# Converting float64 weights with the integer addition and the last subtraction on VectorE instead of GpSimd

## The chip, the cores and the metric

The kernel runs on one core of a Trainium2 chip. The metric is the device time of one execution in microseconds (us); less is better. Engines are named as in the profile: PE is TensorE (matrix products; PEld is its weight load), DVE is VectorE, ACT is ScalarE, POOL is GpSimd, SP is SyncE, which issues all DMAs of this kernel.

## The reference

A two-step attention over packed keys, and then a feed-forward network with a leaky activation, all in float32:

```python
def sm_attn(qq, kk, vv):
    s = scale * np.matmul(qq, kk.transpose(0, 1, 3, 2))
    s = s - np.max(s, axis=-1, keepdims=True)
    a = np.exp(s)
    a = a / (np.sum(a, axis=-1, keepdims=True) + 1e-09)
    return np.matmul(a, vv)
p_packed = sm_attn(p, k, v)            # p: 32 packed queries a head
out = sm_attn(q, p_packed, p_packed)   # back to 576 tokens
...
h = x @ w_in                           # x: out as 4608 tokens x 512
g = np.maximum(h, 0.0) + alpha * np.minimum(h, 0.0)
return (g @ w_out).astype(np.float32)
```

There are 8 batches of 8 heads, 576 tokens, head size 64; the model width is 512, the inner width (`d_ff`) 2048. `w_in` (512 x 2048) and `w_out` (2048 x 512) come as float64 numbers, and the kernel turns them into float32 ones itself.

## The kernel before

Tokens lie on the free axis throughout. `x w_in` is taken as the softmax matrix times `p' w_in`, so that the first product contracts 256 rows. Products are float32 ones made of float32r parts: each operand is split exactly into `hi + lo`, where `hi` is a rounding copy on ACT and `lo` the difference.

**Conversion.** `convert` takes one tile of 128 x 512 float64 numbers from its DMA (`raw`, tile `wraw`) to the pair `hi`, `lo`. There are 32 such units: 16 of `w_in` (made in `packed_w`, result tile `w`, which also goes back to DRAM as `w_split` for later batches) and 16 of `w_out` (made in `load_w_out`, result tile `wo`, which stays). A unit's steps: ACT takes the absolute value of the upper words (L117, `mag`) and scales the lower words to integers (L118, in place in `wraw`); DVE clamps the upper words (L119), moves exponent and fraction to float32's places (L122), and puts the sign on (L128, new tile `full`); POOL adds the lower word as an integer to the bits (L132); ACT makes `hi` (L135); the subtraction that gives `lo` (L137) goes to POOL and to DVE in turn. Raw tiles lie in places of `w_out` that are filled last; four of them rotate. `mag` shares three buffers with the tile `xh`, and `full` three with the tile `xl`, both of `split_x` in the attention.

**Stages.** The first batch's attention comes first, alone. Then the steps of the generators in `plan` are woven into the loop over tiles of the FFN: `first` makes a tile of 128 inner columns by 288 tokens, `second` multiplies it into the four output accumulators two tiles later. In the first batch (32 tiles: both halves over each quarter of `d_ff`) the conversions `w0` and `wo` are woven in, one step of each every two tiles, and DVE makes the activation: `neg` (L490) and `g` (L494) from PSUM. ACT copies `gh` (L505), and `gl` (L507) is the difference, on POOL in the first 48 tiles and on DVE later. Of the attention's other work, POOL has the difference in `split_x` (`xl`, L176), that of v (`vs`, L278), the subtraction of the maximum (L374), the scaling (L381) and `a_l` (L395). Each `g` of the first batch is one instruction of line 494, 32 in all, so their times mark how far the first batch is.

**Order.** The code's order is only a wish: the program is built with a scheduler that reorders the instructions of each engine by its own estimate of times, and then each engine runs its list in order. SP has a list too, so a DMA whose tile is not free holds up those behind it.

Of the kernel before, what the change touches and what calls it, by code (L numbers as in the profile page):

```python
# [8 lines left out]
F32 = mybir.dt.float32  # L9
U32 = mybir.dt.uint32  # L10
U64 = mybir.dt.uint64
F32R = mybir.dt.float32r
AF = mybir.ActivationFunctionType
ALU = mybir.AluOpType
AX = mybir.AxisListType


# Upper words of the float64 numbers 2^-127 and (just under) 2^128, read as float32 numbers.
F64_BOTTOM = float.fromhex("0x1p-15")
F64_TOP = float.fromhex("0x1.dffffep+16")  # L20


def fv(ap):
    """The float32 view of a float32r tile, for reads by the elementwise engines."""
    return ap.bitcast(F32)


# [1 line left out]
def pack_attention_ffn_kernel(  # L29
# [8 lines left out]
    alpha: bass.AP,  # L38
    outT: bass.AP,
):  # L40
    """x = softmax(q p'^T) p' with p' = softmax(p k^T) v, then prelu(x w_in) w_out.

    x w_in is taken as A (p' w_in), A being the softmax over the packed keys, so that
    the first product of the FFN contracts heads * n_pack = 256 rows and not 512.
    Products are float32 ones: each operand is split exactly into two float32r parts
    of 12 significant bits, hi + lo. The small products take all four part products,
    stacked so that they are two passes, the large ones hi*hi + lo*hi + hi*lo.
    Tokens lie on the free axis throughout; the output leaves transposed.
    """
    nc = tc.nc  # L50

    B, NP, P, S = qT.shape
# [13 lines left out]
    xin = ctx.enter_context(tc.tile_pool(name="xin", bufs=3))  # L66
# [3 lines left out]
    at = ctx.enter_context(tc.tile_pool(name="at", bufs=3))  # L70
# [4 lines left out]
    op = ctx.enter_context(tc.tile_pool(name="op", bufs=2))  # L75
# [4 lines left out]

    w_split = dram.tile([NJ, NP, P, 2, 512], F32, name="w_split")

    # ---- constants
    ident = const.tile([P, P], F32, name="ident")
    make_identity(nc, ident)
    ii = const.tile([P, 64], F32, name="ii")
# [6 lines left out]
    pt = const.tile([P, NP, 2, 2, 64], F32R, name="pt")  # L93
# [4 lines left out]
        nc.gpsimd.memset(t, 0.0)  # L98
    wo_t = {}

    turn = [0]
    XF = 1

    def convert(src, raw, place):
        """hi + lo = the float32 nearest to the float64 numbers whose bits are src.

        The upper word carries sign, exponent and 20 bits of the fraction: moved to
        float32's places it is the number cut to 20 bits; 2^exponent times the lower
        word is the rest. The upper word is clamped first to float32's exponents, the
        lowest of which with no fraction stands for zero; sign and top exponent bit do  # L110
        not change by that.
        """
        nc.sync.dma_start(out=raw, in_=src)
        u = raw.bitcast(U32).rearrange("p (f t) -> p f t", t=2)
        up = raw.bitcast(F32).rearrange("p (f t) -> p f t", t=2)[:, :, 1]
        mag = xin.tile([P, 512], F32, name="mag", tag="xh")
        nc.scalar.activation(out=mag, in_=up, func=AF.Abs)  # L117
        nc.scalar.activation(out=u[:, :, 0], in_=u[:, :, 0], func=AF.Copy, scale=2.0**-29)  # L118
        nc.vector.tensor_scalar(  # L119
            out=mag, in0=mag, scalar1=F64_BOTTOM, scalar2=F64_TOP, op0=ALU.max, op1=ALU.min  # L120
        )
        nc.vector.tensor_scalar(  # L122
            out=mag.bitcast(U32), in0=mag.bitcast(U32), scalar1=3, scalar2=0x3FFFFFF8,
            op0=ALU.logical_shift_left, op1=ALU.bitwise_and,
        )
        full = xin.tile([P, 512], F32, name="full", tag="xl")
        bits = full.bitcast(U32)
        nc.vector.scalar_tensor_tensor(  # L128
            out=bits, in0=u[:, :, 1], scalar=0xC0000000, in1=mag.bitcast(U32),
            op0=ALU.bitwise_and, op1=ALU.bitwise_or,  # L130
        )
        nc.gpsimd.tensor_tensor(out=bits, in0=bits, in1=u[:, :, 0], op=ALU.add)  # L132
        hi, lo = place()
        turn[0] += 1
        nc.scalar.copy(out=hi, in_=full)  # L135
        eng = nc.gpsimd if turn[0] % 2 else nc.vector
        eng.tensor_tensor(out=lo, in0=full, in1=fv(hi), op=ALU.subtract)  # L137

    def new_raw(f=0):
        """Room for float64 numbers, in those places of w_out that are filled last."""  # L140
        if f in left:
            left.remove(f)
            n = f
        elif f == NF - 1:
            n = f
        else:
            n = left.pop(0)
            left.append(n)
        return const.tile([P, 512], U64, name=f"wraw{n}", tag=f"wo{n}")
# [9 lines left out]
        raw = new_raw(f)  # L159
        convert(w_out[f * P : (f + 1) * P, :], raw, place)  # L160

    # ---- attention
    def load_x(src, b, pr):
        if b == 0 and (src is kT or pr == NP - 1):
            n = pr if src is kT else 2 * NP
# [24 lines left out]
        return raw  # L190

    def scores(b, pr, st, x, dst, exact):
        """dst[64 rows of this pair] = both heads' scores, keys or tokens on the free axis."""
        ro = (pr % 2) * 64
        for hf in range(2):
            sl = slice(hf * HS, hf * HS + HS)
            if exact:
                if b == 0:
                    tag = f"acc{(2 * pr + hf) % 4}"
                    ps = ps_a.tile([P, 512], F32, name=tag, tag=tag)  # L200
                else:
                    ps = ps_m.tile([P, 512], F32, name="ps_m", tag="m")
                nc.tensor.matmul(ps[:64, :HS], st[:, pr], x[:, sl], start=True, stop=True)
                if hf or b > 0:
                    nc.scalar.copy(out=dst[ro : ro + 64, sl], in_=ps[0:64, :HS])
                else:
                    nc.vector.tensor_copy(out=dst[ro : ro + 64, sl], in_=ps[0:64, :HS])
                continue
            ps = ps_m.tile([P, 512], F32, name="ps_m", tag="m")
            nc.tensor.matmul(ps[:, :HS], st[:, pr], x[0][:, sl], start=True, stop=False)  # L210
            nc.tensor.matmul(ps[:, :HS], st[:, pr], x[1][:, sl], start=False, stop=True)
            lo = sm.tile([64, HS], F32, name="lo", tag="lo", bufs=2)
            nc.scalar.copy(out=lo, in_=ps[64:128, :HS])
            nc.vector.tensor_tensor(
                out=dst[ro : ro + 64, sl], in0=ps[0:64, :HS], in1=lo, op=ALU.add
            )
# [4 lines left out]
        result[b] = (a_h, a_l)  # L221

    def attention(b, tp, exact=False):
        """Steps of two head pairs of a batch; leaves p' in `pt` and the softmax over it in `at`.

        exact takes float32 products as the tensor engine has them: more passes, but no
        splits, for the first batch, before which the tensor engine has nothing to do.
        """
        ptb, slots = (pt0, (0, 1)) if b == 0 else (pt, (b % 2, b % 2))
        pr0, pr1 = prs = (2 * tp, 2 * tp + 1)  # L230
        ts = slice(2 * tp, 2 * tp + 2)
# [1 line left out]
        split = (lambda x: x) if exact else split_x  # L233
# [6 lines left out]
        if tp == 0:  # L240
            for r in range(2):
# [3 lines left out]
                else:  # L245
                    nc.scalar.copy(out=s1[rs, :, 0, cs], in_=praw[rs])
                    nc.vector.tensor_tensor(
                        out=s1[rs, :, 1, cs], in0=praw[rs], in1=fv(s1[rs, :, 0, cs]),
                        op=ALU.subtract,
# [33 lines left out]
        vraw.append(load_v(b, pr1))  # L283
        vs = split_v(0)
        yield
        # rows: keys; columns: pair, (hi, lo), head and packed key
        if exact:
            aT = vin.tile([P, KT, 2, 1, 64], F32, name="aT", tag=("aT", "vs")[tp], bufs=1)
        else:
# [1 line left out]
        for t0 in range(0, KT, 3):  # L291
# [3 lines left out]
            for i in range(n):  # L295
                t = min((t0 + i) * P, S - P)
                nc.tensor.transpose(
                    out=ps[:, i * P : i * P + P], in_=s_t[:, t : t + P], identity=ident
# [3 lines left out]
            if not exact:  # L302
                nc.vector.tensor_tensor(
                    out=aT[:, ks, :, 1, :], in0=psq, in1=fv(aT[:, ks, :, 0, :]), op=ALU.subtract
# [39 lines left out]
        for r in range(2):  # L344
# [3 lines left out]
            else:  # L348
                nc.scalar.copy(out=p2[rs, ts, 0, cs], in_=ppv[rs, :, cs])
                nc.vector.tensor_tensor(  # L350
                    out=p2[rs, ts, 1, cs], in0=ppv[rs, :, cs], in1=fv(p2[rs, ts, 0, cs]),
                    op=ALU.subtract,
                )
        if exact:
            for pr in prs:
                hi, lo = (ptb[:, pr, part, slots[pr % 2], :] for part in range(2))
# [16 lines left out]
        eng = nc.vector if b < 0 else nc.gpsimd  # L373
# [21 lines left out]
        nc.gpsimd.tensor_tensor(out=a_l[:, tp, :], in0=s2, in1=fv(a_h[:, tp, :]), op=ALU.subtract)  # L395
        yield

    # ---- p' w_in for batches of a group, 512 columns of d_ff at a time
    def packed_w(bs, units, fresh=False):
        def get(j, pr):  # L400
            if fresh:
# [48 lines left out]
                ws.append(get(*units[n + LA]))  # L450
            yield

    # ---- FFN of half a batch, one tile of d_ff at a time
    def split_pw(k, h):
        """hi and lo of 256 columns of p' w_in"""
        src = pw[k // 2, h // 2][:, :, (h % 2) * 256 : (h % 2) * 256 + 256]
        th = pwj.tile([P, 2, 256], F32R, name="pwh", tag="pwh")
        tl = pwj.tile([P, 2, 256], F32R, name="pwl", tag="pwl")
        nc.vector.tensor_copy(out=th, in_=src)  # L459
        eng = nc.gpsimd if k < 4 else nc.vector  # L460
        eng.tensor_tensor(out=tl, in0=src, in1=fv(th), op=ALU.subtract)  # L461
        pj[k, h] = (th, tl)
# [117 lines left out]
    for ch in PRO:  # L580
        next(wo if ch == "o" else w0)

    # Work for the gaps: (tile of d_ff from whose loop on it goes, steps, tiles a step)
    A1 = (-1, 6, 19)
    A2 = (17, 20, 30, 34, 40)
    AG = (-8, -5, 12, 15, 30)
# [8 lines left out]
        plan += [(T + AG[n], attention(2 * g + n // 2, n % 2), 1) for n in range(4)]  # L595
        plan += [(T + AG[4], packed_w([2 * g, 2 * g + 1], units(*range(NJ))), 1)]

    # The first batch takes both halves over each quarter of d_ff, whose weights are just then
    # being converted; the others one half after the other over all of it.
    order = [(h, 4 * j + f) for j in range(NJ) for h in range(2) for f in range(4)]  # L600
    order += [(k, f) for k in range(2, 2 * B) for f in range(NF)]
    AHEAD = 2
# [45 lines left out]
```

## Time and profile before

| | before |
|---|---|
| runs, median (lowest to highest) | 849.3 us (848.91 to 850.4) |
| profiled execution, first to last instruction | 849.7 us |
| busy: PE, PEld | 785.0 us (92%), 731.3 us (86%) |
| busy: DVE, ACT, POOL | 661.7 us (78%), 544.3 us (64%), 323.3 us (38%) |
| POOL, additions of the lower word (L132) | 32, 44.2 us |
| POOL, last subtractions into `w` (L137) | 12, 17.8 us |
| moved by DMA | 97.98 MB, mean 115 GB/s |

The profiled execution is one run; its time is its span of 849.7 us, with nothing listed around it, 0.4 us over the median of the three runs. In the rows, "busy" of an engine is the time in which one of its instructions runs, whether that instruction works or stands still; a row of a group gives busy us, mean ns of one, and the idle time ahead with what ended it. A row of the timeline gives the start, the duration and the idle time ahead of it.

### The profile page before, as it was taken

The page shows a single profiled execution, that of the slowest core. Times are in us where ns is not written, and L with a number is a line of the kernel's source. Part 1 is how long each engine was busy: PE and PEld are TensorE (multiplying, and loading weights), DVE is VectorE, ACT ScalarE, POOL GpSimd, SP SyncE. Part 2 cuts the span into 40 slices and gives each one's busy share as a digit, 9 for nine tenths or more (in the row PEclk, how much of TensorE's full clock was granted, in tenths as well). Part 3 has the DMA queues.
Part 4 walks back from the last instruction along what each step waited for, and adds up shares of the span by engine and source line. Part 5 has one row for each costly group of instructions (what it writes and reads, how often), then busy time and mean ns, then how long its engine had stood idle before and what let it go on. Part 6 is the DMA issues. An engine that isn't in the chain of part 4 may idle for free.

```text
span 849.7 us, 15212 instructions
## 1 busy us (share of the span) xinstructions
PE 785.0 (92%) x5384; PEld 731.3 (86%) x5384; DVE 661.7 (78%) x1239; ACT 544.3 (64%) x1333; POOL 323.3 (38%) x299
## 2 busy tenths in 40 slices
PE   5558799998999999999999999998899999999997
PEld 3336668787789999999999999997899999999997
DVE  4999999865788867889989857889889746666663
ACT  5657656547776797666666787656666784545453
POOL 2577768766996621325334402245132100000000
PEclk9869999999999999999999999999999999999999
DMA  8765656445632474222122473221100640000000
GB/s 297 257 225 193 229 188 217 156 145 189 214 109 87 140 244 126 62 57 62 50 59 84 149 234 104 67 70 43 43 15 30 196 154 1 30 1 29 1 30 28
DMA packets 55387, 97.98 MB, mean 115 GB/s; under 512 B 5136, under 2 KB 32784, under 8 KB 55312
## 3 DMA queue, kind: packets, MB, share of 16 engines
q1 hardware_dynamic: 55312, 97.02, 35.6%
q8 instruction: 42, 0.69, 0.3%
q14 instruction: 33, 0.27, 0.1%
HBM read 79.18 MB, written 17.83 MB: 114 GB/s over the span
## 4 chain that ended last, share of the span: by engine, by line
PE 62%; DVE 14%; ACT 5%; issue 3%; DMA 2%; POOL 1%; SPq 0%; DVEq 0%; ACTq 0%; POOLq 0%
PE acc L521 12%; PE acc L519 12%; PE acc L520 12%; PE ps_h L483 6%; PE ps_h L484 5%; PE ps_h L485 5%; DVE g L500 2%; DVE gl L507 2%; DVE pwl L461 2%; DMA outT<-ot 2%; PE ps_m L438 1%; PE ps_m L319 1%; PE ps_m L439 1%; PE ps_m L440 1%; PE ps_m L210 1%
## 5 line engine op out<-in xcount | busy, mean ns | idle before, releaser
L519 PE MATMUL acc<-gh,wo 128*128 128x288 f32 x1024 | 300.5, 302 | 6.3 <-ACT gh L505 2.9
L520 PE MATMUL acc<-gh,wo 128*128 128x288 f32 x1024 | 296.8, 296 | 0.0
L521 PE MATMUL acc<-gl,wo 128*128 128x288 f32 x1024 | 265.3, 298 | 3.7 <-DVE gl L507 2.9
L519 PEld LDWEIGHTS acc<-gh,wo 128*128 128x128 f32 x1024 | 193.4, 189 | 12.9 <-ACT gh L505 3.9
L505 ACT CAST gh<-g 128x288 fp32r<-128x288 f32 x256 | 110.3, 433 | 145.6 <-DVE g L500 105.8
L520 PEld LDWEIGHTS acc<-gh,wo 128*128 128x128 f32 x1024 | 193.5, 189 | 2.2
L521 PEld LDWEIGHTS acc<-gl,wo 128*128 128x128 f32 x1024 | 180.0, 188 | 9.9 <-DVE gl L507 5.0
L507 DVE TENSOR_TENSOR gl<-g,gh 128x288 fp32r<-128x288 f32 x208 | 124.7, 602 | 59.7 <-ACT gh L505 56.5
L500 DVE SCALAR_TENSOR_TENSOR g<-neg,nal,g 128x288 f32<-128x288 f32 x224 | 130.7, 586 | 39.5 <-ACT g L499 38.3
L483 PE MATMUL ps_h<-a_h,pwh 128*128 128x288 f32 x448 | 132.6, 296 | 0.5 <-DVE pwh L459 0.4
L484 PE MATMUL ps_h<-a_l,pwh 128*128 128x288 f32 x448 | 132.0, 295 | 0.0
L485 PE MATMUL ps_h<-a_h,pwl 128*128 128x288 f32 x448 | 131.4, 295 | 0.0
L176 POOL TENSOR_TENSOR xl<-xraw,xh 128x576 fp32r<-128x576 f32 x48 | 72.7, 1514 | 148.5 <-ACT xh L175 144.1
L498 ACT ACTIVATE neg<-ps_h 128x288 f32<-128x288 f32 x224 | 92.2, 412 | 50.4 <-PE ps_h L485 46.6
L499 ACT ACTIVATE g<-ps_h 128x288 f32<-128x288 f32 x224 | 91.0, 408 | 15.0 <-DVE gl L507 13.5
L483 PEld LDWEIGHTS ps_h<-a_h,pwh 128*128 128x128 f32 x448 | 84.2, 188 | 2.0 <-DVE pwh L459 0.7
L484 PEld LDWEIGHTS ps_h<-a_l,pwh 128*128 128x128 f32 x448 | 84.1, 188 | 0.3
L485 PEld LDWEIGHTS ps_h<-a_h,pwl 128*128 128x128 f32 x448 | 83.9, 188 | 0.4
L461 DVE TENSOR_TENSOR pwl<-pw,pwh 128x512 fp32r<-128x512 f32 x96 | 76.1, 793 | 5.7 <-DVE pwh L459 0.5
L459 DVE CAST pwh<-pw 128x512 fp32r<-128x512 f32 x112 | 61.2, 550 | 12.1 <-PE ps_h L484 10.1
L446 ACT COPY pw<-ps_m 64x512 f32<-64x512 f32 x112 | 65.1, 581 | 6.4 <-PE ps_m L440 5.0
L132 POOL TENSOR_TENSOR full<-full,wraw 128x512 uint32<-128x512 uint32 x32 | 44.2, 1382 | 41.2 <-ACT mag L117 14.0
(118 smaller groups left out, 1211.8 us busy)
## 6 DMA issues: line engine op xcount, KB each, us to landing
w<-w_split SPq DMA_DIRECT2D x64, 512.0 KB, 4.1
xraw<-in_kT SPq DMA_DIRECT2D x32, 288.0 KB, 2.9
xraw<-in_qT SPq DMA_DIRECT2D x32, 288.0 KB, 2.9
outT<-ot SPq DMA_DIRECT2D x64, 144.0 KB, 1.8
vraw<-in_v SPq DMA_DIRECT2D x32, 256.0 KB, 2.9
wraw<-in_w_out SPq DMA_DIRECT2D x16, 512.0 KB, 3.7
wraw<-in_w_in SPq DMA_DIRECT2D x16, 512.0 KB, 4.2
w_split<-w SPq DMA_DIRECT2D x16, 512.0 KB, 3.3
```

The source lines that it names most:

```text
L461: eng.tensor_tensor(out=tl, in0=src, in1=fv(th), op=ALU.subtract)
L483: nc.tensor.matmul(ps[:, :HS], th[:, i, fs], a_h[:, i, tok], start=hi, stop=False)
L484: nc.tensor.matmul(ps[:, :HS], th[:, i, fs], a_l[:, i, tok], start=False, stop=False)
L485: nc.tensor.matmul(ps[:, :HS], tl[:, i, fs], a_h[:, i, tok], start=False, stop=lo)
L498: nc.scalar.activation(out=neg, in_=ps[:, :HS], func=AF.Relu, scale=-1.0)
L499: nc.scalar.activation(out=g, in_=ps[:, :HS], func=AF.Relu)
L500: nc.vector.scalar_tensor_tensor(out=g, in0=neg, scalar=nal[:, f : f + 1], in1=g, op0=ALU.mult, op1=ALU.add)
L505: nc.scalar.copy(out=gh, in_=g)
L507: eng.tensor_tensor(out=gl, in0=g, in1=fv(gh), op=ALU.subtract)
L519: nc.tensor.matmul(acc[o][:, :HS], wo_t[f][:, 0, os_], gh, start=begin, stop=False)
L520: nc.tensor.matmul(acc[o][:, :HS], wo_t[f][:, 1, os_], gh, start=False, stop=False)
L521: nc.tensor.matmul(acc[o][:, :HS], wo_t[f][:, 0, os_], gl, start=False, stop=end)
```

## The change

The integer addition moves from POOL to DVE, and all 32 last subtractions are DVE's (16 were). The lower word goes to a tile of its own, `low`, in the buffers that `full` had, instead of being scaled in place; `full` is gone, and `mag` is worked on in place from the absolute value to the last subtraction. The core of the diff (docstrings and comments, which it also takes out, left out here; lines further down move up by three: L490, L494 and L507 are L487, L491 and L504 afterwards):

```diff
-    turn = [0]
...
         mag = xin.tile([P, 512], F32, name="mag", tag="xh")
+        bits = mag.bitcast(U32)
         nc.scalar.activation(out=mag, in_=up, func=AF.Abs)
-        nc.scalar.activation(out=u[:, :, 0], in_=u[:, :, 0], func=AF.Copy, scale=2.0**-29)
+        low = xin.tile([P, 512], U32, name="low", tag="xl")
+        nc.scalar.activation(out=low, in_=u[:, :, 0], func=AF.Copy, scale=2.0**-29)
...
-            out=mag.bitcast(U32), in0=mag.bitcast(U32), scalar1=3, scalar2=0x3FFFFFF8,
+            out=bits, in0=bits, scalar1=3, scalar2=0x3FFFFFF8,
             op0=ALU.logical_shift_left, op1=ALU.bitwise_and,
         )
-        full = xin.tile([P, 512], F32, name="full", tag="xl")
-        bits = full.bitcast(U32)
         nc.vector.scalar_tensor_tensor(
-            out=bits, in0=u[:, :, 1], scalar=0xC0000000, in1=mag.bitcast(U32),
+            out=bits, in0=u[:, :, 1], scalar=0xC0000000, in1=bits,
             op0=ALU.bitwise_and, op1=ALU.bitwise_or,
         )
-        nc.gpsimd.tensor_tensor(out=bits, in0=bits, in1=u[:, :, 0], op=ALU.add)
+        nc.vector.tensor_tensor(out=bits, in0=bits, in1=low, op=ALU.add)
         hi, lo = place()
-        turn[0] += 1
-        nc.scalar.copy(out=hi, in_=full)
-        eng = nc.gpsimd if turn[0] % 2 else nc.vector
-        eng.tensor_tensor(out=lo, in0=full, in1=fv(hi), op=ALU.subtract)
+        nc.scalar.copy(out=hi, in_=mag)
+        nc.vector.tensor_tensor(out=lo, in0=mag, in1=fv(hi), op=ALU.subtract)
```

The scheduler lays the lists anew. In the rows that follow, a number behind `wraw` or `wo` tells one unit's tile from another's. POOL's list from the last copy of the constants on, its first rows before:

```order
L88 COPY ii<-ident 64x64
L132 TENSOR_TENSOR full<-full,wraw_320 128x512
L132 TENSOR_TENSOR full<-full,wraw_333 128x512
L137 TENSOR_TENSOR wo_330<-full,wo_330 128x512
L132 TENSOR_TENSOR full<-full,wraw_347 128x512
L132 TENSOR_TENSOR full<-full,wraw_366 128x512
L137 TENSOR_TENSOR w<-full,w 128x512
L374 TENSOR_TENSOR t_273<-t_273,m_275 128x576
L132 TENSOR_TENSOR full<-full,wraw_380 128x512
L137 TENSOR_TENSOR wo_390<-full,wo_390 128x512
```

and after, down to the first `gl`:

```order
L88 COPY ii<-ident 64x64
L371 TENSOR_TENSOR t_273<-t_273,m_275 128x576
L371 TENSOR_TENSOR t_308<-t_308,m_310 128x576
L378 TENSOR_TENSOR t_273<-t_273,z_288 128x576
L378 TENSOR_TENSOR t_308<-t_308,z_314 128x576
L504 TENSOR_TENSOR gl<-g,gh 128x288 x9
```

Eleven additions and five subtractions stand ahead of the first `gl` before; after, four steps of the attention alone do, and nine of the `gl` follow each other.

DVE's list up to the first `g`, before:

```order
L119 TENSOR_SCALAR mag<-mag 128x512
L122 TENSOR_SCALAR mag<-mag 128x512
L386 STREAM_TRANSPOSE a_f<-t_308 128x576
L137 TENSOR_TENSOR w<-full,w 128x512
L128 SCALAR_TENSOR_TENSOR full<-wraw_460,mag 128x512
L119 TENSOR_SCALAR mag<-mag 128x512
L122 TENSOR_SCALAR mag<-mag 128x512
L490 TENSOR_SCALAR neg<-ps_h,al 128x288
L128 SCALAR_TENSOR_TENSOR full<-wraw_478,mag 128x512
L494 SCALAR_TENSOR_TENSOR g<-ps_h,neg 128x288
```

and after, where `ISA` is the addition of line 131, listed as 1024 elements a partition (the 512 words as halves), and L120, L123, L127 and L134 are the former L119, L122, L128 and L137:

```order
L134 TENSOR_TENSOR w<-mag,w 128x512
L127 SCALAR_TENSOR_TENSOR mag<-wraw_447,mag 128x512
L134 TENSOR_TENSOR w<-mag,w 128x512
L131 ISA mag<-mag,low 128x1024
L120 TENSOR_SCALAR mag<-mag 128x512
L487 TENSOR_SCALAR neg<-ps_h,al 128x288
L120 TENSOR_SCALAR mag<-mag 128x512
L123 TENSOR_SCALAR mag<-mag 128x512
L487 TENSOR_SCALAR neg<-ps_h,al 128x288
L134 TENSOR_TENSOR wo_457<-mag,wo_457 128x512
L491 SCALAR_TENSOR_TENSOR g<-ps_h,neg 128x288
```

Before, eleven units have their sign (L128) ahead of the first `g`; after, nine have, and nine additions and nine subtractions stand there with them, where four subtractions did.

DVE's list up to the 13th `g`, before:

```order
L137 TENSOR_TENSOR wo_881<-full,wo_881 128x512
L128 SCALAR_TENSOR_TENSOR full<-wraw_976,mag 128x512
L490 TENSOR_SCALAR neg<-ps_h,al 128x288
L119 TENSOR_SCALAR mag<-mag 128x512
L494 SCALAR_TENSOR_TENSOR g<-ps_h,neg 128x288
L122 TENSOR_SCALAR mag<-mag 128x512
L128 SCALAR_TENSOR_TENSOR full<-wraw_1060,mag 128x512
L490 TENSOR_SCALAR neg<-ps_h,al 128x288
L119 TENSOR_SCALAR mag<-mag 128x512
L494 SCALAR_TENSOR_TENSOR g<-ps_h,neg 128x288
```

and after:

```order
L127 SCALAR_TENSOR_TENSOR mag<-wraw_839,mag 128x512
L123 TENSOR_SCALAR mag<-mag 128x512
L120 TENSOR_SCALAR mag<-mag 128x512
L131 ISA mag<-mag,low 128x1024
L127 SCALAR_TENSOR_TENSOR mag<-wraw_871,mag 128x512
L123 TENSOR_SCALAR mag<-mag 128x512
L487 TENSOR_SCALAR neg<-ps_h,al 128x288
L131 ISA mag<-mag,low 128x1024
L134 TENSOR_TENSOR w<-mag,w 128x512
L127 SCALAR_TENSOR_TENSOR mag<-wraw_944,mag 128x512
L491 SCALAR_TENSOR_TENSOR g<-ps_h,neg 128x288
```

Ahead of the 13th `g` there stood 24 of L119, 23 each of L122 and L128 and 10 of L137; now there stand 21, 21 and 21 of these, 20 additions and 19 subtractions. Ahead of the 32nd, all 32 units are through DVE's steps on either side. Shortly behind the 32nd, from DVE's row 280 of before (329 of after) on, the two lists agree; so do those of PE, ACT and SP from places near it.

## The prediction

> **What bounds the kernel now.** First the page's slices, which show the change's stage, then busy times by stretch, then what PE waits for, last single instructions on DVE and POOL. The slices are 21 us each:
>
> ```profile
> span 849.7 us, 15212 instructions
> PE   5558799998999999999999999998899999999997
> DVE  4999999865788867889989857889889746666663
> POOL 2577768766996621325334402245132100000000
> ```
>
> PE is full from the fifth slice or so; before that DVE is at nine tenths, POOL at seven, and PE at five. The next rows cut this at the 13th and the 32nd `g` of line 494 (PE, PEld, DVE, ACT, POOL in order); the last row is the long stage behind.
>
> ```profile
> 17.00:108.50 91.50, 62.91 (x294) 45.43 (x293) 90.50 (x132) 60.18 (x135) 63.64 (x51) 0.87 0.69 231
> 108.50:187.00 78.50, 73.90 (x416) 59.75 (x415) 66.26 (x126) 42.90 (x94) 55.37 (x51) 0.98 0.53 179
> ...
> 280.00:850.00 570.00, 553.19 (x4044) 542.08 (x4042) 428.84 (x843) 367.42 (x926) 126.37 (x111) 1.00 0.25 77
> ```
>
> In the first half of the conversions DVE is busy 90.50 of 91.50 us: its list of instructions is the clock, and PE waits for it. In the second half DVE has 12.2 us free and PE is busy 73.9 of 78.5; behind 280 us PE is the bound at 97%. What PE waits for in the first half:
>
> ```profile
> PE ps_h L471 <- DVE g L494: 9.5, 4, 3.1
> PE ps_m L440 <- DVE w L137: 6.1, 2, 3.1
> PE ps_m L438 <- ACT w L135: 6.0, 1, 6.0
> ```
>
> All three are conversion results, or stand behind conversions in DVE's list. Whether DVE's 90.50 us is work is told by 4 us of both engines, DVE first, then POOL:
>
> ```profile
> 68.60 0.42 DVE L119 TENSOR_SCALAR mag<-mag 128x512 f32<-128x512 f32 x1
> 69.05 1.43 DVE L122 TENSOR_SCALAR mag<-mag 128x512 uint32<-128x512 uint32 x1
> 70.40 1.28 DVE L137 TENSOR_TENSOR wo<-full,wo 128x512 fp32r<-128x512 f32 x1
> 71.61 0.68 DVE L128 SCALAR_TENSOR_TENSOR full<-wraw,mag 128x512 uint32<-128x512 uint32 x1
> 72.21 0.41 DVE L119 TENSOR_SCALAR mag<-mag 128x512 f32<-128x512 f32 x1
> 72.54 0.50 DVE L490 TENSOR_SCALAR neg<-ps_h,al 128x288 f32<-128x288 f32 x1
> ...
> 68.76 1.44 POOL L132 TENSOR_TENSOR full<-full,wraw 128x512 uint32<-128x512 uint32 x1 [1.32 <-PE ps_h L471]
> 70.15 0.98 POOL L507 TENSOR_TENSOR gl<-g,gh 128x288 fp32r<-128x288 f32 x1
> ```
>
> Beside POOL's addition of 1.44 us, L122 takes 1.43, though the same form took 0.43 at 17.53 us (row below); beside `gl` L507, the subtraction L137 takes 1.28. With POOL idle at 71.61 to 72.42, DVE goes through at 0.68 and 0.41, and each starts 0.60 and 0.33 behind the one ahead. So DVE stands still while POOL runs, and the profile calls that busy. My clean prices are 0.42 for the two TENSOR_SCALARs, 0.68 for the two-input forms (0.33 and 0.60 from start to start).
>
> ```profile
> 17.07 0.43 DVE L119 TENSOR_SCALAR mag<-mag 128x512 f32<-128x512 f32 x1 [2.36 <-ACT mag L117]
> 17.53 0.43 DVE L122 TENSOR_SCALAR mag<-mag 128x512 uint32<-128x512 uint32 x1
> 108.50 0.44 DVE L494 SCALAR_TENSOR_TENSOR g<-ps_h,neg 128x288 f32<-128x288 f32 x1
> 186.09 0.46 DVE L494 SCALAR_TENSOR_TENSOR g<-ps_h,neg 128x288 f32<-128x288 f32 x1
> ```
>
> **The change part by part.** DVE's list is the path, so I count it to the 13th `g` (108.5 us) and on to the 32nd (186.1). Conversions stand all within; behind, the orders agree.
>
> *Blocking that goes, first half.* Groups of that stretch, mean ns behind the comma:
>
> ```profile
> L128 DVE SCALAR_TENSOR_TENSOR full<-wraw,mag 128x512 uint32<-128x512 uint32 x23 | 22.6, 982 | 0.4
> L122 DVE TENSOR_SCALAR mag<-mag 128x512 uint32<-128x512 uint32 x23 | 21.8, 947 | 0.3
> L119 DVE TENSOR_SCALAR mag<-mag 128x512 f32<-128x512 f32 x24 | 18.5, 772 | 2.4 <-ACT mag L117 2.4
> L137 DVE TENSOR_TENSOR wo<-full,wo 128x512 fp32r<-128x512 f32 x6 | 7.3, 1224 | 0.0
> L137 DVE TENSOR_TENSOR w<-full,w 128x512 fp32r<-128x512 f32 x4 | 4.3, 1080 | 0.0
> ...
> L507 POOL TENSOR_TENSOR gl<-g,gh 128x288 fp32r<-128x288 f32 x11 | 11.5, 1042 | 0.0
> L374 POOL TENSOR_TENSOR t<-t,m 128x576 f32<-128x576 f32 x2 | 3.0, 1492 | 1.4 <-DVE m L372 1.4
> L381 POOL TENSOR_TENSOR t<-t,z 128x576 f32<-128x576 f32 x2 | 2.5, 1246 | 0.5 <-ACT mag L117 0.5
> ```
>
> Above the clean prices stand 23 x 0.30 = 6.9, 23 x 0.53 = 12.1, 24 x 0.35 = 8.4, 6 x 0.54 = 3.3 and 4 x 0.40 = 1.6 us: 32.4, or 0.51 us for each us that POOL is busy (63.64). POOL keeps 11.5 + 3.0 + 2.5 = 17.0 us of that, which at 0.51 still block 8.7. Ends: 0.25 (half the rate, as shorter instructions fit more often beside DVE's reads of PSUM) gives 4.3, a full 1.0 gives 17.0.
>
> *Work that comes, first half.* By the order, 20 additions and 9 more subtractions stand ahead of the 13th `g`, and 3 fewer L119, 2 fewer L122 and 2 fewer L128. The addition (`ISA`) is not in the trace; its nearest row is L128, two 32-bit streams of 512 in, one out. So 29 x 0.60 = 17.4, less 5 x 0.33 and 2 x 0.60: +14.5. Ends of an addition: 0.33, as a TENSOR_SCALAR, and 1.2, if its 1024 halves go one at a time. The Trainium skill, "VectorE: DVE Perf Modes", section Mode 2×_1P, has 16-bit streams of unit step pass two a cycle; 512 pairs there are worth about 0.53 us and a fixed part, an estimate by that page which would leave the sum where it is; no run here shows it yet.
>
> First half: 14.5 - 32.4 + 8.7 = **-9.2 us** (-13.6 to -0.9 by the blocking rate).
>
> *Second half.* The rows of that stretch:
>
> ```profile
> L128 DVE SCALAR_TENSOR_TENSOR full<-wraw,mag 128x512 uint32<-128x512 uint32 x9 | 9.1, 1006 | 0.2
> L119 DVE TENSOR_SCALAR mag<-mag 128x512 f32<-128x512 f32 x8 | 6.7, 835 | 3.3 <-ACT mag L117 3.2
> L122 DVE TENSOR_SCALAR mag<-mag 128x512 uint32<-128x512 uint32 x9 | 6.6, 732 | 0.1
> L137 DVE TENSOR_TENSOR wo<-full,wo 128x512 fp32r<-128x512 f32 x6 | 5.8, 971 | 0.0
> ...
> L507 POOL TENSOR_TENSOR gl<-g,gh 128x288 fp32r<-128x288 f32 x20 | 17.0, 851 | 15.4 <-ACT gh L505 13.5 <-PE acc L521 1.9
> L176 POOL TENSOR_TENSOR xl<-xraw,xh 128x576 fp32r<-128x576 f32 x6 | 8.8, 1460 | 1.2 <-DVE wo L137 0.6 <-ACT xh L175 0.6
> L395 POOL TENSOR_TENSOR a_l<-s,a_h 128x576 fp32r<-128x576 f32 x2 | 3.3, 1661 | 0.0
> L374 POOL TENSOR_TENSOR t<-t,m 128x576 f32<-128x576 f32 x2 | 2.3, 1157 | 0.4 <-DVE m L372 0.4
> L381 POOL TENSOR_TENSOR t<-t,z 128x576 f32<-128x576 f32 x2 | 2.3, 1154 | 0.0
> L278 POOL TENSOR_TENSOR vs<-vraw,vs 128x640 fp32r<-128x640 f32 x1 | 2.0, 2027 | 0.0
> ```
>
> Blocked: 9 x 0.33 + 8 x 0.42 + 9 x 0.31 + 6 x 0.29 = 10.8 us, only 0.20 per us of POOL (55.37), since DVE is not full. The other 19 new instructions and the postponed ones come here: 11.4 + 2.9 = 14.3. POOL keeps 17.0 + 8.8 + 3.3 + 2.3 + 2.3 + 2.0 = 35.7 us. DVE, fuller than before, will be blocked at a rate between 0.20 and 0.51; I take 0.33, as DVE's share of conversions lies between the halves': 11.8 (7.1 to 18.2). DVE then needs 66.3 - 10.8 + 14.3 + 11.8 = 81.6, and some 3 of its 12.2 idle us are waits for ACT and PE that stay: 84.6 against 78.5, so **+6.1**. DVE takes over from PE as this half's bound.
>
> *POOL and ACT.* POOL loses 48 instructions and no longer makes `gl` wait behind a 1.4 us addition: nothing on the path, as POOL's end is not waited for once DVE is late. ACT does the same three steps a unit; the lower word goes to a tile of its own, at the same size. Buffers: `mag` now lives until the last subtraction, with three of them. A unit takes 91.5 / 23 = 4.0 us of DVE's time in turn, so the fourth waits only if a unit takes over 12 us; its own DVE steps are 0.33 x 2 + 0.60 x 3 = 2.5. The eight-odd us of queueing cover it; without them ACT would wait with `gh` behind it. The DMA for a raw tile can go earlier, since the tile is free after L128 and not after POOL's addition: free here, as DVE has units waiting. Behind 187 us the rows are the same: 0.
>
> Sum: -9.2 + 6.1 = -3.1. Against the profiled 849.7 that is 846.6; the median of the runs shown is 849.3, 0.4 lower, so **846.3 us**.
>
> **The rivals.**
> *The second half eats it all* (slower): POOL's remaining instructions block at the first half's 0.51 there, 18.2 us, and 5 us of waits stay. DVE needs 66.3 - 10.8 + 14.3 + 18.2 + 5 = 93.0, +14.5, net +5.3: 855. It decides from a rate of about 0.42, where 69.8 + 3 + 35.7 x 0.42 = 87.7 uses up the lead. For it: DVE will be as full as in the first half. Against: its work there is less of two-input forms.
> *The lead stays*: blocking at 0.20, DVE needs 76.9 and PE's 73.9 bounds, so the half takes its 78.5: about 840. For it: PE's row there. Against: no waits would be left on DVE.
> *A wash*: the short `gl` blocks for its whole length, as 0.60 of 0.98 us in the row at 70.15 already suggests: a lead of 1 to 5, all given back, 849.
> *The addition takes 1.2 us*: 32 x 0.6 = +19 on a full DVE, 865.
> *Busy is work*: if DVE's long instructions are merely slow, nothing is freed: +14.5, and 14.3 less 12.2 idle: 866. The trace bears little of it (0.41 and 0.68 with POOL idle). This is what the Trainium skill, "Perfetto Trace Analysis", section Identifying the Most-Contended Engine, would make of it: it takes occupancy as the measure for Vector, by which work is moved on to the fullest engine.
>
> **How the numbers follow.** Forecast 0.34 (843 to 849.5), second half eats it 0.24, lead stays 0.14, wash 0.20, slow addition 0.05, busy is work 0.03. A measurement tells 0.2%, 1.7 us, from no change. Faster: 0.30 of the forecast, 0.14, and 0.04 of the wash: 0.48. Same: 0.03 and 0.14: 0.17, and 0.02 of the slower rival: 0.19. Slower: 0.33. The range, 839 to 857, leaves out the last two cases and the ends of the rates. The faster case's own range is 840 to 847.
>
> **What would show it.** L120 and L123 near 0.42 and L127 near 0.68 in the mean, `ISA` near 0.68; the 13th `g` near 99 us (95 to 108); DVE busy over 95% up to about 180 us; the 32nd `g` near 183; a distance from there to the end of 663 us as now. Wrong if the 13th `g` is not earlier, if `ISA` takes over 1 us, or if DVE's forms stay long beside `gl`.

## The result, and the profile after

| | before | after |
|---|---|---|
| runs, median (lowest to highest) | 849.85 us (848.91 to 851.45), 4 runs | 843.5 us (843.26 to 844.03), 4 runs |
| profiled execution, span | 849.7 us | 842.0 us |
| ratio to before, 95% interval | | 0.992 [0.9903, 0.9937] |
| POOL busy, whole span | 323.3 us | 260.1 us |
| DVE busy, whole span | 661.7 us, 1239 instructions | 661.8 us, 1287 instructions |

The changed kernel is 0.8% faster; the forecast was 846.3 us. The medians differ by 6.35 us, twice the forecast's 3.1. The profiled execution of after took 844.03 us as timed, 2.0 us more than its span, so spans are set against spans here (-7.7 us). Wherever a run's time and span are both on record, the time is 1.7 to 2.1 us above the span. By that the profiled execution of before, with its span of 849.7 us, was not 0.4 us over the median but near 851.5 us as timed, like the slowest of the four (851.45); so a part of the -7.7 us comes from which executions were profiled.

The head and the slices of the page of after, 21 us each:

```profile
span 842.0 us, 15167 instructions
PE   5489989898999999998999999997999999999997
DVE  4999999965788857889989848889889656666663
POOL 2122234667895511344335302244232100000000
```

PE is fuller from the third slice to the fifth (8 9 9, before 5 8 7) and a little emptier behind (8 9 8 9 8, before 9 9 9 9 8): a lead is won and partly given back. DVE's row is as full as it was, and POOL's second to fifth slices have 1 or 2 tenths instead of 5 to 7. The stretches, cut as before at the first conversion, the 13th `g`, the 32nd `g`, and 272 us (PE, PEld, DVE, ACT, POOL):

```profile
16.60:96.50 79.90, 63.99 (x316) 46.24 (x315) 78.55 (x154) 56.06 (x122) 18.28 (x18) 0.87 0.73 242
96.50:178.00 81.50, 73.39 (x393) 57.93 (x393) 76.09 (x151) 47.14 (x104) 37.12 (x35) 0.96 0.58 190
272.00:842.00 570.00, 555.45 (x4045) 545.25 (x4044) 429.83 (x843) 367.36 (x926) 126.46 (x111) 0.99 0.25 77
```

The 13th `g` comes at 96.5 us instead of 108.5, the 32nd at 177.8 instead of 186.1. In the first half DVE runs 154 instructions where it ran 132, and is busy 78.55 us where it was 90.50, though two units fewer have their sign by then (21, before 23). Up to the 32nd, where all units are through on either side, it runs 305 instructions by these rows, before 258, in 7.9 us less. In the second half it is busy 76.09 of 81.50 us. From there to the end it is 664.2 us; before it was 663.6. DVE's groups of the first half:

```profile
L131 DVE CUSTOM_DVE_ANT_0 mag<-mag,low 128x1024 uint16<-128x1024 uint16 x20 | 15.9, 801 | 0.0
L127 DVE SCALAR_TENSOR_TENSOR mag<-wraw,mag 128x512 uint32<-128x512 uint32 x21 | 15.0, 719 | 0.0
L123 DVE TENSOR_SCALAR mag<-mag 128x512 uint32<-128x512 uint32 x21 | 10.6, 510 | 0.1
L120 DVE TENSOR_SCALAR mag<-mag 128x512 f32<-128x512 f32 x21 | 9.4, 451 | 2.7 <-ACT mag L117 2.7
L134 DVE TENSOR_TENSOR w<-mag,w 128x512 fp32r<-128x512 f32 x11 | 7.7, 696 | 0.0
L134 DVE TENSOR_TENSOR wo<-mag,wo 128x512 fp32r<-128x512 f32 x8 | 7.0, 874 | 0.0
```

The first row is the new addition; as 1024 halves it is 801 ns in the mean. The three steps that both kernels have fell from 982 to 719 (sign), from 947 to 510 (shift) and from 772 to 451 ns (clamp). Single instructions show the clean prices and what is still held up, DVE first, then POOL:

```profile
59.43 0.68 DVE L131 CUSTOM_DVE_ANT_0 mag<-mag,low 128x1024 uint16<-128x1024 uint16 x1
60.82 0.67 DVE L134 TENSOR_TENSOR wo<-mag,wo 128x512 fp32r<-128x512 f32 x1
61.42 0.68 DVE L127 SCALAR_TENSOR_TENSOR mag<-wraw,mag 128x512 uint32<-128x512 uint32 x1
62.39 0.91 DVE L134 TENSOR_TENSOR w<-mag,w 128x512 fp32r<-128x512 f32 x1
63.23 1.33 DVE L131 CUSTOM_DVE_ANT_0 mag<-mag,low 128x1024 uint16<-128x1024 uint16 x1
64.48 0.41 DVE L120 TENSOR_SCALAR mag<-mag 128x512 f32<-128x512 f32 x1
...
61.74 1.01 POOL L504 TENSOR_TENSOR gl<-g,gh 128x288 fp32r<-128x288 f32 x1 [2.52 <-ACT gh L502]
63.20 0.81 POOL L504 TENSOR_TENSOR gl<-g,gh 128x288 fp32r<-128x288 f32 x1 [0.44 <-ACT gh L502]
```

With POOL idle the addition and the subtraction take 0.68 and 0.67 us and the clamp 0.41; the sign, which starts 0.32 us ahead of a `gl`, takes 0.68. Beside a `gl` the addition at 63.23 takes 1.33. What DVE waits for in the second half, before and then after (us in total, times, longest):

```profile
DVE mag L119 <- ACT mag L117: 3.2, 3, 1.7
DVE s_t L214 <- ACT lo L213: 3.1, 3, 1.2
```

```profile
DVE s_t L211 <- ACT lo L210: 0.5, 1, 0.5
DVE mag L120 <- ACT mag L117: 0.2, 1, 0.2
```

Both waits for ACT are nearly gone there; DVE has more work ahead of them in its list, which would explain it.

### The profile page after: what moved, and what is told of

It is laid out like the page before. It is cut to its first block, busy times and chain, and to the rows that moved or that the text cites. A ratio compares the mean times of both kernels' runs of the same rounds, so it can differ in the third digit from the quotient of the medians.

```text
span 842.0 us, 15167 instructions
## 1 busy us (share of the span) xinstructions
PE 788.6 (94%) x5384; PEld 733.9 (87%) x5384; DVE 661.8 (79%) x1287; ACT 545.1 (65%) x1333; POOL 260.1 (31%) x251
## 4 chain that ended last, share of the span: by engine, by line
PE 69%; DVE 16%; ACT 6%; DMA 4%; issue 3%; POOL 1%; SPq 1%; ACTq 0%; DVEq 0%; POOLq 0%
PE acc L516 13%; PE acc L518 13%; PE acc L517 13%; PE ps_h L482 6%; PE ps_h L480 6%; PE ps_h L481 6%; DVE g L497 2%; PE ps_h L468 2%; PE ps_m L435 2%; DVE gl L504 1%; PE ps_m L437 1%; PE ps_m L316 1%; PE ps_m L436 1%; DVE mag L127 1%; DVE pwl L458 1%
## 5 line engine op out<-in xcount | busy, mean ns | idle before, releaser
L516 PEld LDWEIGHTS acc<-gh,wo 128*128 128x128 f32 x1024 | 193.1, 189 | 15.3 <-ACT gh L502 6.2
L504 DVE TENSOR_TENSOR gl<-g,gh 128x288 fp32r<-128x288 f32 x208 | 123.9, 598 | 60.3 <-ACT gh L502 56.8
L497 DVE SCALAR_TENSOR_TENSOR g<-neg,nal,g 128x288 f32<-128x288 f32 x224 | 133.5, 598 | 38.1 <-ACT g L496 36.9
L496 ACT ACTIVATE g<-ps_h 128x288 f32<-128x288 f32 x224 | 91.1, 408 | 14.5 <-DVE gl L504 12.9
L504 POOL TENSOR_TENSOR gl<-g,gh 128x288 fp32r<-128x288 f32 x48 | 45.0, 947 | 68.1 <-ACT gh L502 65.0
```

The costliest lines, as they stand in the source:

```text
L496: nc.scalar.activation(out=g, in_=ps[:, :HS], func=AF.Relu)
L497: nc.vector.scalar_tensor_tensor(out=g, in0=neg, scalar=nal[:, f : f + 1], in1=g, op0=ALU.mult, op1=ALU.add)
L504: eng.tensor_tensor(out=gl, in0=g, in1=fv(gh), op=ALU.subtract)
L516: nc.tensor.matmul(acc[o][:, :HS], wo_t[f][:, 0, os_], gh, start=begin, stop=False)
```

## The experiments

"Before" of each comparison ran on the same chip: 850.7, 850.09 and 850.16 us in the three sets. "After" ran in a set of its own (before 849.85), so a difference from it goes across sets. Window rows are cut at the first conversion, the 13th and the 32nd `g`, so their bounds are those times; the columns are as above.

**The subtractions alone on DVE**

```diff
-        eng = nc.gpsimd if turn[0] % 2 else nc.vector
-        eng.tensor_tensor(out=lo, in0=full, in1=fv(hi), op=ALU.subtract)
+        nc.vector.tensor_tensor(out=lo, in0=full, in1=fv(hi), op=ALU.subtract)
```

> The kernel before, with only the 16 last subtractions of POOL moved to DVE; the 32 additions stay on POOL and the buffers are those of before. Theory P (POOL's instructions hold DVE up, and that is what the change takes away): 23 of 67 us of POOL's conversion work go, so a third of the gain, -2 us (-4 to +1), and DVE's L119, L122, L128 get shorter by about a third of their excess (L122 from 0.89 to about 0.75 us). Rival O (the gain comes from the new buffers and the list that the scheduler makes of them): no gain, 849.5 +- 1.5. Rival L (the gain is the shorter chain of a unit, addition on DVE in 0.7 us instead of 1.4 on POOL): no gain, since the addition stays.

Measured: 857.86 us, ratio 1.0086 [1.0066, 1.0105]. Every theory missed. The two halves, then groups of all units:

```profile
16.60:113.40 96.80, 69.67 (x327) 50.33 (x325) 95.76 (x150) 63.57 (x138) 51.68 (x42) 0.85 0.71 233
113.40:192.90 79.50, 72.68 (x392) 57.40 (x393) 65.81 (x126) 42.24 (x94) 47.39 (x44) 0.96 0.51 166
```

```profile
L128 DVE SCALAR_TENSOR_TENSOR full<-wraw,mag 128x512 uint32<-128x512 uint32 x32 | 31.3, 977 | 0.2
L122 DVE TENSOR_SCALAR mag<-mag 128x512 uint32<-128x512 uint32 x32 | 24.7, 776 | 0.2
L119 DVE TENSOR_SCALAR mag<-mag 128x512 f32<-128x512 f32 x32 | 20.9, 654 | 6.1 <-ACT mag L117 6.1
L136 DVE TENSOR_TENSOR w<-full,w 128x512 fp32r<-128x512 f32 x16 | 15.8, 994 | 0.6 <-ACT w L135 0.6
L136 DVE TENSOR_TENSOR wo<-full,wo 128x512 fp32r<-128x512 f32 x16 | 15.3, 958 | 0.7 <-ACT wo L135 0.7
L132 POOL TENSOR_TENSOR full<-full,wraw 128x512 uint32<-128x512 uint32 x32 | 45.5, 1423 | 55.7 <-DVE full L128 18.5 <-ACT c L323 13.5 <-issue 7.5
```

The shift and the clamp get shorter, as theory P had it (776 and 654 ns, before 886 and 788 over all units), and the sign stays long (977, before 989): together some 8 us less. But the additions are still POOL's, and beside its remaining instructions DVE's subtractions take 994 and 958 ns; they cost DVE 31.1 us instead of 17.5. So DVE is busy 161.6 us up to the 32nd `g`, 5.6 more than before. Theory P had left out what the subtractions cost on DVE. This half of the change costs 7 us if done by itself.

**The additions alone on DVE** (the changed kernel with the last subtractions in turn again)

```diff
-        nc.vector.tensor_tensor(out=lo, in0=mag, in1=fv(hi), op=ALU.subtract)
+        turn[0] += 1
+        eng = nc.gpsimd if turn[0] % 2 else nc.vector
+        eng.tensor_tensor(out=lo, in0=mag, in1=fv(hi), op=ALU.subtract)
```

> The changed kernel, but the last subtractions go to POOL and DVE in turn as before; only the 32 additions have moved, with the new buffers. P: 44 of 67 us of POOL's conversion work are gone, two thirds of the gain, -4 us (-7 to -1). L: the whole gain, -6 us, as the additions are the long step of the chain. O: the whole gain, as the buffers are the new ones.

Measured: 847.11 us, 0.9957 [0.9942, 0.9971]: 3.6 us faster than before, as expected of blocking; L and O had asked for the whole gain. The two halves:

```profile
16.80:107.20 90.40, 70.09 (x325) 49.38 (x323) 88.92 (x156) 61.50 (x135) 34.85 (x29) 0.85 0.71 240
107.20:183.70 76.50, 69.52 (x384) 56.10 (x385) 71.31 (x138) 45.19 (x100) 48.52 (x43) 0.98 0.55 184
```

By the ratios (0.9957 and 0.992) the subtractions bring another 3 us from here to the full change, where they cost 7 by themselves. So the two parts don't add up. The first halves are not alike (23 units have their sign ahead of the 13th `g` here, 21 in after), so the sums up to the 32nd are compared: DVE is busy 160.2 us here and 154.6 in after, though it runs 11 instructions more there (305 and 294), and POOL's 83.4 us go down to 55.4.

**The buffers alone** (the kernel above with the addition back on POOL; so `low` has its own tile, `full` is gone, and both engines' work is that of before)

```diff
-        nc.vector.tensor_tensor(out=bits, in0=bits, in1=low, op=ALU.add)
+        nc.gpsimd.tensor_tensor(out=bits, in0=bits, in1=low, op=ALU.add)
```

> The buffers of the changed kernel (own tile for the lower word, bits worked on in place) with the engines of before: 32 additions and 16 subtractions on POOL. P and L: no gain, 849.5 +- 2, L122 about 0.89 us as before. O: the gain is here, 843 to 845.

Measured: 856.14 us, 1.0064 [1.0046, 1.0082]; all expectations missed. What ACT waits for in the conversions:

```profile
ACT mag L118 <- DVE wo L137: 7.5, 6, 2.4
ACT mag L118 <- DVE w L137: 3.7, 3, 1.9
```

and in the changed kernel:

```profile
ACT mag L117 <- DVE w L134: 1.9, 3, 1.5
ACT mag L117 <- DVE wo L134: 1.7, 4, 0.6
```

Before has no such row; its `mag` waits for DMAs alone. With the three `mag` buffers held until the last subtraction, ACT waits 11.2 us for DVE, and the time grows by 5.4. The rows fit the buffers as the cause, but the scheduler's list is another one too, and no run separates the two. With the addition and all subtractions on DVE, 3.6 us of that wait are left; with the additions alone (the kernel ahead of this one) 6.3, and 2.7 for POOL's subtractions. Moving the addition (this kernel to the one ahead of it) is thus worth 9.0 us, of which the new buffers had cost 5.4. So it was partly luck that theory P's -4 was met there: it had put the buffers at nothing.

**POOL's time put back, DVE's work kept** (per unit a dead addition on POOL, whose result nobody reads, beside the changed kernel)

```diff
+    dead = const.tile([P, 512], U32, name="dead")
...
         nc.vector.tensor_tensor(out=bits, in0=bits, in1=low, op=ALU.add)
+        nc.gpsimd.tensor_tensor(out=dead, in0=low, in1=low, op=ALU.add)
```

> The changed kernel with one more POOL addition a unit (32 in all, 128x512, both inputs the tile of the lower word, result never read). It leaves DVE's work and the chain of a unit as they are and puts 44 us of POOL back beside them. P: DVE's L120, L123, L127 and the addition get long again (TENSOR_SCALAR of bits from 0.60 to about 0.9 us in the mean), DVE loses 0.3 to 0.5 us for each us of POOL, 13 to 22 us, and the time is 852 to 862. L and O: POOL has room for it, 843.5 +- 2.

Measured: 861.49 us, 1.0134 [1.011, 1.0158]. The two halves, then three groups of all units:

```profile
16.90:110.30 93.40, 70.50 (x327) 49.35 (x325) 93.10 (x157) 57.30 (x127) 47.34 (x40) 0.85 0.64 207
110.30:194.10 83.80, 71.34 (x367) 55.02 (x368) 79.84 (x146) 46.85 (x101) 49.59 (x46) 0.94 0.55 177
```

```profile
L133 POOL TENSOR_TENSOR dead<-low 128x512 uint32<-128x512 uint32 x32 | 41.4, 1294 | 62.5 <-ACT low L120 47.7 <-ACT c L323 12.7 <-PE acc L520 1.9
L128 DVE SCALAR_TENSOR_TENSOR mag<-wraw,mag 128x512 uint32<-128x512 uint32 x32 | 29.9, 935 | 0.1
L121 DVE TENSOR_SCALAR mag<-mag 128x512 f32<-128x512 f32 x32 | 21.4, 669 | 3.4 <-ACT mag L118 3.3
```

DVE has the same instructions as after, with as many of each conversion step ahead of the 13th and of the 32nd `g`, and 93.10 + 79.84 = 172.9 us of them instead of 154.6. That is 18.3 us more for 41.4 us of additions, 0.44 us per us, and the time is 18 us above after's; the sign has 935 ns (after 756 over all units), the clamp 669 (478), the addition 888 (780), while the shift, expected near 0.9 us, stays at 612 (602). Nothing waits for `dead`, so a chain that passes it can't be the reason, and PE waits only 1.8 us for `gl`, which queues behind it on POOL. This shows the blocking by itself. The rate of 0.51 read from the profile before belongs to another mix of instructions.

**A POOL instruction that only writes** (the changed kernel, and the raw tile set to zero on POOL once a unit is through with it)

```diff
         nc.vector.tensor_tensor(out=bits, in0=bits, in1=low, op=ALU.add)
+        nc.gpsimd.memset(raw.bitcast(U32), 0)
```

> The changed kernel with one POOL memset a unit over its raw tile once the tile is read (32 in all, 128x1024, about 0.95 us each, nothing reads the zeros): POOL is busy again for 30 us, but it reads nothing, where the dead additions read two inputs. Theory A (any POOL instruction holds DVE up): all of DVE's conversion forms get longer as with the dead additions, 0.3 to 0.46 us for each us of POOL, +9 to +14, 853 to 858. Theory R (it takes POOL's reads for the forms with two inputs; only the one-input TENSOR_SCALARs, L120 and L123, meet a memset too): the bits' L127, the addition and L134 stay near 0.76 to 0.81, L120 and L123 rise by 0.1 to 0.2, +3 to +7, 847 to 851, of which up to 3 are the raw tiles that come free later.

Measured: 855.23 us, 1.0065 [1.0048, 1.0082]. The time falls in the range of the one theory and the rows speak for the other. POOL, then DVE, at three places:

```profile
21.83 1.14 POOL L132 MEMSET wraw<- 128x1024 uint32 x1 [2.19 <-ACT aT L299]
26.08 0.95 POOL L132 MEMSET wraw<- 128x1024 uint32 x1 [3.12 <-ACT mag L117]
32.87 0.95 POOL L132 MEMSET wraw<- 128x1024 uint32 x1 [2.73 <-ACT pw L440]
...
22.01 1.23 DVE L120 TENSOR_SCALAR mag<-mag 128x512 f32<-128x512 f32 x1
26.59 0.65 DVE L135 TENSOR_TENSOR w<-mag,w 128x512 fp32r<-128x512 f32 x1
33.11 0.99 DVE L123 TENSOR_SCALAR mag<-mag 128x512 uint32<-128x512 uint32 x1
```

The TENSOR_SCALARs at 22.01 and 33.11 end 0.3 us behind the memset beside them; the subtraction at 26.59, with two inputs, runs through one. Over all instructions that have a memset and no other POOL instruction beside them for over 0.2 us, the clamp has a mean of 1.02 us (6: four of 1.23 to 1.59, two of 0.41) and the shift 0.85 (2), while the sign has 0.68 (2), the addition 0.72 (10, one of them 1.12, behind a TENSOR_SCALAR that stood) and the subtraction 0.67 (5). By the Trainium skill, "SBUF — State Buffer", section Who interferes with whom, a two-input instruction of VectorE competes with GpSimd's reads alone, and a one-input form in a two-port mode with any GpSimd instruction; these rows agree.

The total is no measure of that: a raw tile now comes free only after the memset, and SP's list waits for it (100 to 230 us; total, times, longest):

```profile
SPq L112 <- POOL wraw L132: 18.6, 6, 7.1
```

PE has run 668 matmuls by the 32nd `g` here and 709 in after, so part of the delay shows only behind that mark. Up to it DVE is busy 160.8 us, 6.1 more than in after; over all units the clamp's mean rises from 478 to 673 ns, the shift's does not rise (602 to 564), and the sign's and the addition's rise by about 50. How much of the 11.7 us is blocking and how much the DMAs stays open.

**`gl` of the first batch on DVE as well** (it stays on POOL in tiles 32 to 47)

```diff
-        eng = nc.gpsimd if 0 <= i < 48 else nc.vector
+        eng = nc.gpsimd if 32 <= i < 48 else nc.vector
```

> The changed kernel, with gl of the first batch's 32 tiles on DVE as well (from tile 32 to 47 it stays on POOL). By the price of the runs so far: 30 us of POOL go, which hold DVE for about 0.3 us each us, -9; 32 differences of 288 elements come to DVE at 0.38 from start to start, +12: 846.5 (844 to 850). Rival: the shorter way to gl lets PE go on sooner, and DVE has idle time in the second half, so 841 to 843.

Measured: 846.97 us, 0.9965 [0.9952, 0.9978], as the sum had it (846.5), and 3.5 us behind after. The two halves:

```profile
17.10:93.30 76.20, 60.27 (x299) 44.13 (x299) 75.57 (x162) 54.28 (x123) 5.57 (x6) 0.87 0.74 239
93.30:181.60 88.30, 76.79 (x409) 61.05 (x408) 83.44 (x175) 51.33 (x108) 20.98 (x16) 0.94 0.59 192
```

The 13th `g` is 3.2 us earlier and the 32nd 3.8 later; DVE's busy time in both together is 159.0 us, in after 154.6. So a `gl` on POOL holds DVE up for less than it costs on DVE: the move pays down to a point, and this is past it.

**More raw tiles in the kernel before**

```diff
-    SPARE = 4
+    SPARE = 6
```

> The kernel before with six rotating places for raw tiles and not four. DVE's idle time before the 32nd g was 13 us before and 6.7 with the additions on DVE. Theory W (part of that is conversions that wait for a raw tile which POOL's addition holds): more places take 3 us or more of it, 845 to 848, and the wait of mag on its DMA goes. Rival F (the idle time went since DVE had more to do and so filled it): no gain, 849.5 +- 2.

Measured: 855.18 us, 1.0059 [1.0045, 1.0073]; both expectations missed. The two halves:

```profile
17.00:120.90 103.90, 72.01 (x328) 49.19 (x326) 101.03 (x150) 67.15 (x146) 71.47 (x57) 0.84 0.71 237
120.90:189.50 68.60, 66.30 (x373) 54.60 (x374) 51.53 (x108) 37.44 (x82) 45.63 (x45) 0.98 0.47 153
```

With raw tiles at hand the scheduler puts more conversions ahead of the first `g` (14 clamps, before 11), which comes at 66.8 us instead of 59.5, and the 13th comes 12 us later. So raw tiles that come free earlier don't explain the gain: given in this way, which also changes the order, they cost time.

**The activation of some of the first 32 tiles shared with ACT** (changed kernel; the other branch is the one of later tiles: two ACT instructions and one of DVE in place of two of DVE). Half of them:

```diff
-        if 0 <= i < 32:
+        if 0 <= i < 32 and i % 2 == 0:
```

> The changed kernel, with ACT making the two halves of the activation in every other tile of the first batch, as it does in all later tiles, so that DVE has one instruction of 0.45 us there and not two of 0.80. If DVE's list is still the clock up to the 32nd g: 16 x 0.35 = 5.6 us less on DVE, 838 to 841. If ACT (0.64 busy there, 13 us more) or the chain over ACT is the clock: 843 to 847.

Then three quarters (`i % 4 == 0` stays DVE's) and all:

> The changed kernel, with the activation of 24 of the first 32 tiles as in the later tiles (ACT makes the two halves, DVE one instruction) instead of 16 of them. With 16, DVE lost 4.2 us of busy time and the time fell by about 2.2 us against the changed kernel. If DVE's list is still the clock of the first batch, eight more bring about another 1 us: 839.5 to 841.5. If the result of ACT is now what g waits for (ACT gets 3.3 us more, and gh stands behind it), it stays where it was or is lost again: 842 to 846.

> The same with all 32 tiles. If DVE's list is the clock: 838 to 841. If ACT takes over as what is waited for: 843 to 848, with waits of DVE's line 497 for ACT's line 496 in the first batch.

Measured: 841.35 us (0.99 [0.9886, 0.9915]), 841.7 (0.9897 [0.988, 0.9913]) and 842.33 (0.9905 [0.9887, 0.9922]). Each lies between the two ranges that were named for it, so neither theory is met as stated. Half of the tiles bring about 2 us against after, though the intervals overlap, and the rest nothing more. From 17 to 180 us DVE is busy 154.9 us in after, then 154.4, 153.1 and 147.8 (the window is fixed, and DVE runs 305, 295, 283 and 273 instructions in it); with all tiles, its waits rise instead:

```profile
DVE mag L120 <- ACT mag L117: 6.4, 4, 2.7
DVE g L497 <- ACT g L496: 2.4, 5, 1.1
```

This is the kernel with all tiles from 17 to 185 us; in after the first of these waits is 2.9 us and the second can't be. By these rows a part of what DVE no longer does is now waited for from ACT. These three are the fastest versions, and the differences between them lie within the scatter of their runs.

## Why the prediction was right, and where its steps were off

- **DVE is held up by POOL: right.** It runs 22 more instructions in the first half and is busy 11.95 us less; the dead additions bring the loss back (172.9 us instead of 154.6). The rival *busy is work* (866) falls with that.
- **Work that comes, +14.5: right.** 20 additions and 9 more subtractions stood in the first half. The clean addition is 0.68 us, the price of L128; *the slow addition* (865) falls. The Trainium skill's rate, two 16-bit elements a cycle ("VectorE: DVE Perf Modes", section Mode 2×_1P), gave an estimate of 0.53 us and a fixed part, and the row of 0.68 agrees with it.
- **Blocking that is left in the first half, 8.7 us for 17.0 of POOL: nearly right.** Above the clean prices stand 20 x 0.12 + 21 x 0.04 + 21 x 0.09 + 21 x 0.03 + 11 x 0.02 + 8 x 0.19 = 7.5 us, 0.41 per us of POOL's 18.28.
- **First half, -9.2: -11.6 in length (91.50 to 79.90 us).** The sum with 7.5 gives -10.4. What it left out are other DVE forms that POOL also held: the small `z` TENSOR_SCALARs lose 0.8 us. The remaining 0.4 us isn't assigned.
- **Second half, +6.1: +3.7** (77.6 to 81.3 us). DVE was forecast 15.3 us busier and is 10.4 (65.5 to 75.9, both cut at the 32nd `g` itself). Blocking left is 10.0 us instead of 11.8, the rate 0.27 per us of POOL instead of 0.33; other forms lose 2.0 (L358's `pt` alone 1.8), which I had counted as work; some 1 us isn't assigned. Against that, 5.4 us of idle time stay where I kept 3: `ot` waits 2.4 us for its DMA, which I had not counted. So within this half two errors partly cancel. Both halves were sized 2.4 us too high; with the start 0.4 us earlier and the end 0.6 longer that makes the 4.6 us by which the span was missed (-3.1 forecast, -7.7 measured). The direction was right; the forecast's size is half of what came.
- **Part of the lead is given back: right, but less than forecast.** The forecast gives back 6.1 of 9.2 us, two thirds; 3.7 of 11.6 were, a third. The lead is 12.0 us at the 13th `g` (96.5 us, forecast near 99) and 8.3 at the 32nd (177.8, forecast near 183). So *the second half eats it all* and *a wash* fall, and *the lead stays* too (its 840 asks for a second half no longer than before); the time lies about midway between its 840 and the forecast. DVE as the bound there is half right: 93% busy, not the 95% that I named (96% over both halves together), and PE at 90%.
- **L120 and L123 near 0.42, L127 near 0.68: only in part.** Over the 32 units the means are 0.48, 0.60 and 0.76, and 0.78 for the addition; in the second half L123 has 0.78, with `gl` and `xl` beside it. Forms that stay long beside `gl` were named as a sign of being wrong, and that sign did show (the addition at 63.23); the sum had priced it, at 0.51 and 0.33 us per us of POOL, and 0.41 and 0.27 came.
- **Buffers free: wrong by themselves.** They cost 5 us with the engines of before, and I had argued that queueing covers them. In the changed kernel ACT's wait for `mag` is 3.6 us instead of 11.2, and what is left of their cost can't be told from the rest. That a unit's shorter chain on DVE frees them sooner fits the rows and isn't shown.
- **Behind 187 us, 0: right**, 664.2 against 663.6 us. With +0.6 there the sum is -12.0 + 3.7 + 0.6 = -7.7 us of span.

## What to carry to other kernels

A busy engine may be standing still: compare one form's durations with the neighbour idle and with it running before moving work, since here DVE ran 47 more instructions up to the 32nd `g` in 7.9 us less. The parts of such a move need not add up, so each is tried alone and together: the subtractions cost 7 us while the additions were POOL's, the additions with the new buffers won 3.6, both won 6.3. Why the subtractions pay only then isn't shown, since additions and buffers both changed in between. The move stops paying where the moved instruction costs more than it blocked (`gl`: 3.5 us lost). What was tried next, a third engine with time to spare, brought about 2 us, which is at the edge of the scatter.

## What was not expected of the hardware

A POOL instruction that only writes can hold up DVE's TENSOR_SCALARs (0.41 us alone, 1.23 to 1.59 in four of six clamps) but not its two-input forms (0.68 alone, 0.65 to 0.68 beside a memset, but for one addition); a POOL addition or subtraction can hold up both, as the shift of 1.43 and the subtraction of 1.28 in the prediction's rows show. How much DVE loses per us of POOL differed: 0.44 with the dead additions, 0.41 in the first half of after, 0.27 in the second. That the forms which happen to meet make this difference is likely and not shown.
